# Token mixing in two halves of the features, interleaved with the output projection

## The chip, the cores and the metric

The kernel runs on one core of a Trainium2 chip. The metric is the device time of one execution in microseconds (us). Five engines work beside each other and meet at semaphores: TensorE (PE; its weight loads are listed as PEld), VectorE (DVE), ScalarE (ACT), GpSimd (POOL) and SyncE (SP), which issues DMAs.

## The reference

Three layers follow each other, for 4 batches of 576 tokens and 512 features (8 heads of 64):

```
scores = q @ k.T / sqrt(D) + min(-(cum[i] - cum[j]), 0), causal   # cum = cumsum(relu(s))
x      = softmax(scores) @ v                                      # heads side by side: (B, 576, 512)
gate   = sigmoid(causal conv of x over 5 tokens, per feature)
x      = (gate * (x @ w_val)) @ w_out
h      = x.T @ U @ V          # token mixing: U is 576 x 32, V is 32 x 576
u      = x + h.T
out    = u + relu(u @ w_ch1) @ w_ch2                              # 512 -> 2048 -> 512
```

Everything is float32. The large products are made of fp32r pieces: a value is split into a rounded high part and a rest, and three products (high with high, high with rest, rest with high) are added in PSUM.

## The kernel before, in words

Features lie on the partitions. uT holds the whole activation as 4 tiles of 128 features by 2304 tokens. The work has three stages. First attention: 32 heads in a software pipeline (the loop at line 762), scores of head n beside the transposes and products of head n - 1. After each pair of heads `norm` (590) scales the accumulator av, of which there is one buffer (pool psV), and five conv taps and a tanh (609 to 622) overwrite it and read it. Second, for each batch, `dense_work` (640): `values` (645) makes gate times the value projection, split into gvh and gvl per tile of 128 features and half of the tokens; `outputs` (668) makes the output projection and then the token mixing. Third, the two-layer MLP (865 to 933).

`outputs` first loops over the two halves of 288 tokens and, inside, over the 4 feature tiles m; each of these 8 output tiles is 12 matmuls of 288 columns (`products`, 627), and ACT writes it to uT (kind "ox"). Then comes token mixing, for the 5 chunks of 128 tokens (the last overlaps): four PE transposes bring the chunk of all 512 features into one PSUM bank (686 to 690), ACT rounds it to nh, DVE makes the rest nl, and two matmuls of 512 columns add U times nh and U times nl into the bank acc (699, 700). The sum is split into the tile `a` (named ast): ACT rounds it, DVE makes the rest of its lower half (703, 704). Last, 16 matmuls of 288 columns multiply with V, and DVE adds each result to uT (706 to 713). nh and nl have one buffer each, and ast uses nh's.

What sets the order: these functions are generators. Each `yield` names a cost on a planner's clock, and between two yields the caller puts other work. For batches 0 to 2 the caller is `run_dense` (751), which spreads a batch's dense work over the attention of the next batch, at a budget (DENSE = 36.0) divided by the heads that are left. For batch 3 it is `beside` (943), which puts 0.4 of a piece of the MLP's first blocks behind each yield and 6 pieces behind the yield of the value LULL. `defer` (156) emits a step some time later on that clock, `force` (160) at once; `until` (184) moves the clock on until a step has been emitted. At the end a list scheduler orders each engine's instructions by a simulated time and by priorities that the table PLAN (23) gives to each kind of step; the kind "tm" (the mixing's matmuls and transposes) goes 6000 places ahead. All matmul results of the three stages except av and two MLP accumulators share one pool of 6 PSUM banks, psD (225).

Of the kernel before, what the change touches and what calls it, by code (L numbers as in the profile page):

```python
# [11 lines left out]
F32 = mybir.dt.float32  # L12
F32R = mybir.dt.float32r
# [78 lines left out]
DT = {"exp": 0.51, "xh": 0.96, "xl": 0.25, "tap": 1.5, "taps": 0.9, "tanh": 1.83, "gv": 4.3, "nl": 3.6, "rows": 10.0, "prep": 1.51}  # L92
# [4 lines left out]
def fused_kernel(ctx, tc, qT, kT, vP, s, wval, wout, convw, U, V, w1, w2, rows01, out):  # L97
    nc = tc.nc
    B, H, D, S = qT.shape
    P = 128  # L100
    NP = H // 2
    NT = B * S
    HS = S // 2
# [31 lines left out]
    def rnd(kind, o, i, by=1.0):  # L135

        eng = Via(kind)
        if eng.name == "scalar":
            eng.mul(o, i, by)  # L139
        elif eng.name == "vector" and by == 1.0:  # L140
            eng.tensor_copy(o, i)
        else:
            eng.tensor_scalar(o, i, by, 0.0, op0=ALU.mult, op1=ALU.add)  # L143

    def rest(kind, o, i, hi, by=1.0):

        if by == 1.0:
            Via(kind).tensor_sub(o, i, hi.bitcast(F32))
        else:
            Via(kind).scalar_tensor_tensor(o, i, by, hi.bitcast(F32), op0=ALU.mult, op1=ALU.subtract)  # L150
# [5 lines left out]
    def defer(dt, f, key=None):  # L156
        order[0] += 1
        later.append((clock["now"] + dt, order[0], f, key))

    def force(key, keep=0):  # L160

        held = sorted((x for x in later if x[3] == key), key=lambda y: y[:2])
        for x in held[:max(0, len(held) - keep)]:
            later.remove(x)
            x[2]()
# [18 lines left out]
    def until(*keys):  # L184

        while any(k not in ready for k in keys):
            assert later
            advance(0.1)
# [12 lines left out]
    uT = left.tile([P, NP, NT], F32, name="uT")  # L201
# [425 lines left out]
    def products(o, w, m, hi, lo):  # L627

        K = len(hi)
        for kc in range(K):  # L630
            wh = w["h"][:, kc, m * P:(m + 1) * P]
            Via("d").matmul(o, wh, hi[kc], start=(kc == 0), stop=False)
            Via("d").matmul(o, wh, lo[kc], start=False, stop=False)
            Via("d").matmul(o, w["l"][:, kc, m * P:(m + 1) * P], hi[kc], start=False, stop=(kc == K - 1))
            yield 0.37
# [32 lines left out]
    def outputs(b):  # L668
        halves = [slice(0, HS), slice(HS, S)]
        need(*[("wide", c) for c in range(NP, 2 * NP)])  # L670
        for hf, cols in enumerate(halves):
            for m in range(NP):
                until(*[("gv", b, p, hf) for p in range(NP)])
                ps = psD.tile([P, 512], F32, tag="d", name="d")
                yield from products(
                    ps[:, 0:HS], wo, m, [gvh[p, hf] for p in range(NP)], [gvl[p, hf] for p in range(NP)],
                )
                rnd("ox", uT[:, m, b * S + hf * HS:b * S + hf * HS + HS], ps[:, 0:HS], 0.5)
        yield 0.0
        need(*[("wide", c) for c in range(2 * NP, len(wide))])  # L680
        acc = psD.tile([P, 512], F32, tag="d", name="d")
        for c in range(5):
            s0 = b * S + min(c * P, S - P)
            force("pt", 1)
            if b < B - 1:
                ps = psD.tile([P, 512], F32, tag="d", name="pt")
            else:
                ps = psD.tile([P, 512], F32, tag="d", name="d")
            for m in range(NP):
                Via("tm").transpose(ps[:, m * P:(m + 1) * P], uT[:, m, s0:s0 + P], ident)  # L690
            nh = da.tile([P, 512], F32R, tag="nh", name="nh")
            nl = da.tile([P, 512], F32R, tag="nl", name="nl")
            rnd("nh", nh, ps)
            defer(DT["nl"], lambda ps=ps, nh=nh, nl=nl: rest("nl", nl, ps, nh), "pt")
            yield 0.44
            yield 0.8
            force("pt")
            lhsT = U4[:, c, :, :].rearrange("p a r -> p (a r)")
            Via("tm").matmul(acc, lhsT, nh, start=(c == 0), stop=False)
            Via("tm").matmul(acc, lhsT, nl, start=False, stop=(c == 4))  # L700
            yield 0.44
        a = da.tile([P, 512], F32R, tag="nh", name="ast")
        rnd("ah", a, acc)
        rest("al", a[64:, :], acc[64:, :], a[64:, :])
        yield LULL
        for m in range(NP):
            for hf, cols in enumerate(halves):
                ps = psD.tile([P, 512], F32, tag="d", name="d")
                lhsT = a[:, m * P:(m + 1) * P]
                Via("tm").matmul(ps[:, 0:HS], lhsT, V4["h"][:, cols], start=True, stop=False)  # L710
                Via("tm").matmul(ps[:, 0:HS], lhsT, V4["l"][:, cols], start=False, stop=True)
                u = uT[:, m, b * S + hf * HS:b * S + hf * HS + HS]
                Via("um").tensor_add(u, ps[:, 0:HS], u)
                yield 0.25

# [299 lines left out]
```

## Time and profile before

| | us |
|---|---|
| median of 3 timed runs | 756.13 (754.95 to 756.43) |
| the profiled execution | 759.41 |
| its span, first to last instruction | 757.3 |

| engine | busy us | share of the span |
|---|---|---|
| PE | 733.2 | 97% |
| PEld | 617.8 | 82% |
| DVE | 473.0 | 62% |
| POOL | 337.8 | 45% |
| ACT | 264.5 | 35% |

Busy time is an average over stages that differ. By the instructions of the trace, attention runs up to about 319 us, the dense work of batch 3 from there to about 380 us, and the MLP alone after that. The ends of matmuls in a profile are modelled, so that a wait of PE can be somewhat longer than the idle time listed. The granted clock is given as a share of 2.4 GHz.

### The profile page before, as it was taken

The numbers are of one execution on the slowest core, as the hardware profiler recorded it, in microseconds if no ns is written. First come the engines' busy times: TensorE is split into PE (matmuls) and PEld (weight loads), VectorE is DVE, ScalarE is ACT, GpSimd is POOL, SyncE is SP. The second block draws the span as 40 slices with busy tenths as digits, with TensorE's granted clock in tenths as the row PEclk, the third lists the DMA queues.
The fourth block names the chain that finished last, engine by engine and source line by source line (L and its number), as shares of the span: only waits on it lengthen the run. The fifth ranks groups of instructions, "written<-read, shape, count | busy, mean of one in ns | idle before, by whom it ended". The sixth has DMA issues, their size and how long they took to land.

```text
span 757.3 us, 12161 instructions
## 1 busy us (share of the span) xinstructions
PE 733.2 (97%) x4369; PEld 617.8 (82%) x4369; DVE 473.0 (62%) x1053; ACT 264.5 (35%) x718; POOL 337.8 (45%) x393
## 2 busy tenths in 40 slices
PE   8988999899999999999999999999999999999998
PEld 5756889688887998798788888888888888888887
DVE  6888887987668656752548899864572234223234
ACT  6767656745677567622110110110011011001110
POOL 2677677555544243650097787732660024100000
PEclk9999999999999999999999999999999999999999
DMA  4665454645555431110002222210120000000033
GB/s 120 192 186 141 104 141 117 167 117 141 119 140 137 113 97 43 46 57 1 0 29 84 84 84 84 84 55 29 57 85 0 1 29 1 0 1 1 0 112 139
DMA packets 27000, 59.39 MB, mean 78 GB/s; under 512 B 4648, under 2 KB 5288, under 8 KB 26940
## 3 DMA queue, kind: packets, MB, share of 16 engines
q1 hardware_dynamic: 26940, 58.61, 27.8%
q8 instruction: 35, 0.57, 0.3%
q14 instruction: 25, 0.20, 0.1%
HBM read 37.04 MB, written 5.31 MB: 56 GB/s over the span
## 4 chain that ended last, share of the span: by engine, by line
PE 85%; DVE 8%; issue 2%; DMA 2%; ACT 2%; POOL 1%; ACTq 0%; DVEq 0%; POOLq 0%
PE d L132 39%; PE acc L132 26%; PE pt L132 8%; PE av L132 6%; PE sc L132 5%; DVE P L132 2%; DVE uT L132 2%; DVE av L614 2%; DMA uT<-in_w 1%; ACT P L132 0%; DMA K<-Q 0%; DVE nl L132 0%; POOL uT L143 0%; DVE uT L313 0%; ACT PTB L132 0%
## 5 line engine op out<-in xcount | busy, mean ns | idle before, releaser
L132 PE MATMUL d<-u,w1h 128*128 128x512 f32 (+1 forms) x640 | 184.4, 371 | 0.0
L877 ACT ACTIVATE hh<-d 128x512 fp32r<-128x512 f32 (+1 forms) x80 | 44.3, 556 | 342.8 <-PE acc L132 173.8
L132 DVE SCALAR_TENSOR_TENSOR hl<-d,hh 128x512 fp32r<-128x512 f32 (+1 forms) x80 | 50.5, 634 | 147.2 <-ACT hh L877 147.0
L132 PEld LDWEIGHTS d<-u,w1h 128*128 128x128 f32 x640 | 116.0, 188 | 22.4
L132 PE MATMUL d<-u,w1l 128*128 128x512 f32 (+1 forms) x320 | 118.5, 371 | 0.0
L132 PE MATMUL acc<-hl,w2h 128*128 128x512 f32 (+1 forms) x320 | 104.5, 370 | 0.0
L132 PE MATMUL acc<-hh,w2h 128*128 128x512 f32 (+1 forms) x320 | 104.3, 371 | 0.2 <-DVE uT L132 0.2
L132 ACT ACTIVATE P<-P,nm 128x576 f32<-128x576 f32 (+4 forms) x160 | 89.1, 560 | 36.9 <-DVE nm L132 36.3
L132 PE MATMUL acc<-hh,w2l 128*128 128x512 f32 (+1 forms) x320 | 101.1, 369 | 0.0
L132 PE MATMUL sc<-K,Q 68*128 68x288 f32 (+13 forms) x384 | 87.8, 343 | 2.3 <-ACT PTA L139 1.5
L132 DVE TENSOR_TENSOR uT<-acc,uT 128x512 f32<-128x512 f32 (+1 forms) x120 | 70.1, 628 | 31.6 <-PE acc L132 31.5
L132 DVE CUSTOM_DVE_ANT_0 P<-sc,causal 64x64 f32<-64x64 f32 (+4 forms) x160 | 64.9, 420 | 26.4 <-PE sc L132 22.3
L132 PE MATMUL pt<-ident,P 128*128 128x128 f32 x480 | 75.6, 282 | 5.0 <-ACT P L132 3.0
L132 PEld LDWEIGHTS sc<-K,Q 68*128 68x128 f32 (+2 forms) x384 | 62.8, 194 | 9.7 <-ACT PTA L139 2.0
L132 PEld LDWEIGHTS d<-u,w1l 128*128 128x128 f32 x320 | 60.3, 188 | 11.2
L132 PEld LDWEIGHTS acc<-hh,w2h 128*128 128x128 f32 x320 | 58.8, 188 | 11.5 <-issue 0.6
L132 PEld LDWEIGHTS acc<-hl,w2h 128*128 128x128 f32 x320 | 58.9, 188 | 10.9 <-DVE hl L132 0.3
L132 PEld LDWEIGHTS acc<-hh,w2l 128*128 128x128 f32 x320 | 58.7, 188 | 10.6
L132 PEld LDWEIGHTS pt<-ident,P 128*128 128x128 f32 x480 | 54.4, 142 | 13.5 <-ACT P L132 5.4
L132 DVE SCALAR_TENSOR_TENSOR scr<-raw,scr 128x512 uint32<-128x512 uint32 (+1 forms) x56 | 55.7, 995 | 1.4
L132 DVE TENSOR_SCALAR scr<-scr 128x512 uint32<-128x512 uint32 x56 | 44.7, 798 | 17.9 <-POOL scr L375 9.7
L614 DVE SCALAR_TENSOR_TENSOR av<-X,cw,av 128x576 f32<-128x576 f32 x64 | 52.1, 814 | 3.0 <-ACT av L132 2.7
(124 smaller groups left out, 1274.3 us busy)
## 6 DMA issues: line engine op xcount, KB each, us to landing
raw<-in_w SPq DMA_DIRECT2D x28, 512.0 KB
K<-hi SPq DMA_DIRECT2D x44, 144.0 KB
Q<-hi SPq DMA_DIRECT2D x44, 144.0 KB
V<-in_vP SPq DMA_DIRECT2D x16, 320.0 KB
out<-uT SPq DMA_DIRECT2D x16, 256.0 KB
qk<-in_qT SPq DMA_DIRECT2D x22, 144.0 KB
qk<-in_kT SPq DMA_DIRECT2D x22, 144.0 KB
K<-Q SPq DMA_DIRECT2D x22, 144.0 KB
```

The lines of the kernel that those rows point to most:

```text
L132: return f(*args, **kw)
L614: Via("tap").scalar_tensor_tensor(g, X[:, k:k + S], cw[:, p, k:k + 1], g, op0=ALU.mult, op1=ALU.add,)
L877: Via("hh").activation(h_, o, AF.Relu)
```

## The change

`outputs` becomes three inner generators: `output(m, hf)` for one output tile, `mix(f)` for the mixing of one half of the features (two tiles, 256 columns), and `back(f)` for that half's products with V. In `mix` two chunks of tokens share one PSUM bank of transposes and one tile nh and nl (chunks 0 and 1, 2 and 3, then 4 alone); the products with U take 256 columns each. Each half has its own tile ast. The output tiles of the first two feature tiles come first, for both halves of the tokens; the first mixing steps once behind every second product of the other four output tiles; the second mixing starts with three steps that yield nothing and then steps once behind each product pair of `back(0)`. The yield of LULL and `back(1)` come last. The second yield of a chunk costs 0.6 in place of 0.8.

```diff
@@ -668,50 +668,83 @@
     def outputs(b):
         halves = [slice(0, HS), slice(HS, S)]
         need(*[("wide", c) for c in range(NP, 2 * NP)])
-        for hf, cols in enumerate(halves):
-            for m in range(NP):
-                until(*[("gv", b, p, hf) for p in range(NP)])
-                ps = psD.tile([P, 512], F32, tag="d", name="d")
-                yield from products(
-                    ps[:, 0:HS], wo, m, [gvh[p, hf] for p in range(NP)], [gvl[p, hf] for p in range(NP)],
-                )
-                rnd("ox", uT[:, m, b * S + hf * HS:b * S + hf * HS + HS], ps[:, 0:HS], 0.5)
-        yield 0.0
+        def output(m, hf):
+            until(*[("gv", b, p, hf) for p in range(NP)])
+            ps = psD.tile([P, 512], F32, tag="d", name="d")
+            yield from products(
+                ps[:, 0:HS], wo, m, [gvh[p, hf] for p in range(NP)], [gvl[p, hf] for p in range(NP)],
+            )
+            rnd("ox", uT[:, m, b * S + hf * HS:b * S + hf * HS + HS], ps[:, 0:HS], 0.5)
+        W = NP // 2 * P
+        asts = {}
+        def mix(f):
+            ms = range(f * NP // 2, (f + 1) * NP // 2)
+            acc = psD.tile([P, 512], F32, tag="d", name="d")[:, 0:W]
+            for cs in ((0, 1), (2, 3), (4,)):
+                w = W * len(cs)
+                force("pt", 1)
+                if b < B - 1:
+                    ps = psD.tile([P, 512], F32, tag="d", name="pt")
+                else:
+                    ps = psD.tile([P, 512], F32, tag="d", name="d")
+                for k, (c, m) in enumerate((c, m) for c in cs for m in ms):
+                    s0 = b * S + min(c * P, S - P)
+                    Via("tm").transpose(ps[:, k * P:(k + 1) * P], uT[:, m, s0:s0 + P], ident)
+                nh = da.tile([P, 512], F32R, tag="nh", name="nh")
+                nl = da.tile([P, 512], F32R, tag="nl", name="nl")
+                rnd("nh", nh[:, 0:w], ps[:, 0:w])
+                defer(DT["nl"], lambda: rest("nl", nl[:, 0:w], ps[:, 0:w], nh[:, 0:w]), "pt")
+                yield 0.44
+                yield 0.6
+                force("pt")
+                for k, c in enumerate(cs):
+                    lhsT = U4[:, c, :, :].rearrange("p a r -> p (a r)")
+                    cols = slice(k * W, (k + 1) * W)
+                    Via("tm").matmul(acc, lhsT, nh[:, cols], start=(c == 0), stop=False)
+                    Via("tm").matmul(acc, lhsT, nl[:, cols], start=False, stop=(c == 4))
+                yield 0.44
+            a = asts[f] = da.tile([P, W], F32R, tag=f"ast{f}", name="ast")
+            rnd("ah", a, acc)
+            rest("al", a[64:, :], acc[64:, :], a[64:, :])
+        def back(f):
+            for k in range(NP // 2):
+                m = f * NP // 2 + k
+                for hf, cols in enumerate(halves):
+                    ps = psD.tile([P, 512], F32, tag="d", name="d")
+                    lhsT = asts[f][:, k * P:(k + 1) * P]
+                    Via("tm").matmul(ps[:, 0:HS], lhsT, V4["h"][:, cols], start=True, stop=False)
+                    Via("tm").matmul(ps[:, 0:HS], lhsT, V4["l"][:, cols], start=False, stop=True)
+                    u = uT[:, m, b * S + hf * HS:b * S + hf * HS + HS]
+                    Via("um").tensor_add(u, ps[:, 0:HS], u)
+                    yield 0.25
+        for hf in range(2):
+            for m in range(NP // 2):
+                yield from output(m, hf)
         need(*[("wide", c) for c in range(2 * NP, len(wide))])
-        acc = psD.tile([P, 512], F32, tag="d", name="d")
-        for c in range(5):
-            s0 = b * S + min(c * P, S - P)
-            force("pt", 1)
-            if b < B - 1:
-                ps = psD.tile([P, 512], F32, tag="d", name="pt")
-            else:
-                ps = psD.tile([P, 512], F32, tag="d", name="d")
-            for m in range(NP):
-                Via("tm").transpose(ps[:, m * P:(m + 1) * P], uT[:, m, s0:s0 + P], ident)
-            nh = da.tile([P, 512], F32R, tag="nh", name="nh")
-            nl = da.tile([P, 512], F32R, tag="nl", name="nl")
-            rnd("nh", nh, ps)
-            defer(DT["nl"], lambda ps=ps, nh=nh, nl=nl: rest("nl", nl, ps, nh), "pt")
-            yield 0.44
-            yield 0.8
-            force("pt")
-            lhsT = U4[:, c, :, :].rearrange("p a r -> p (a r)")
-            Via("tm").matmul(acc, lhsT, nh, start=(c == 0), stop=False)
-            Via("tm").matmul(acc, lhsT, nl, start=False, stop=(c == 4))
-            yield 0.44
-        a = da.tile([P, 512], F32R, tag="nh", name="ast")
-        rnd("ah", a, acc)
-        rest("al", a[64:, :], acc[64:, :], a[64:, :])
+        first = mix(0)
+        for hf in range(2):
+            for m in range(NP // 2, NP):
+                for i, cost in enumerate(output(m, hf)):
+                    yield cost
+                    if i % 2:
+                        yield next(first, 0.0)
+        yield from first
+        second = mix(1)
+        for _ in range(3):
+            yield next(second)
+        for cost in back(0):
+            yield cost
+            yield next(second, 0.0)
+        yield from second
         yield LULL
-        for m in range(NP):
-            for hf, cols in enumerate(halves):
-                ps = psD.tile([P, 512], F32, tag="d", name="d")
-                lhsT = a[:, m * P:(m + 1) * P]
-                Via("tm").matmul(ps[:, 0:HS], lhsT, V4["h"][:, cols], start=True, stop=False)
-                Via("tm").matmul(ps[:, 0:HS], lhsT, V4["l"][:, cols], start=False, stop=True)
-                u = uT[:, m, b * S + hf * HS:b * S + hf * HS + HS]
-                Via("um").tensor_add(u, ps[:, 0:HS], u)
-                yield 0.25
+        yield from back(1)
```

## Rows read from the trace of the kernel before

**Rows 1.** The page: PE's busy share, and the chain that ended last.
```profile
PE 733.2 (97%) x4369; PEld 617.8 (82%) x4369; DVE 473.0 (62%) x1053; ACT 264.5 (35%) x718; POOL 337.8 (45%) x393
...
PE 85%; DVE 8%; issue 2%; DMA 2%; ACT 2%; POOL 1%; ACTq 0%; DVEq 0%; POOLq 0%
```

**Rows 2.** Windows, columns as headed: outputs and mixing of batches 0 to 3.
```profile
core 0: us, PE busy (x) PEld busy (x) DVE busy (x) ACT busy (x) POOL busy (x), PEclk, DMA share, GB/s
...
131.90:160.90 29.00, 27.02 (x188) 20.60 (x186) 25.34 (x72) 19.04 (x55) 14.89 (x23) 0.94 0.58 148
188.60:215.90 27.30, 26.55 (x210) 24.55 (x209) 18.87 (x58) 18.22 (x55) 16.06 (x21) 1.00 0.46 113
215.90:242.00 26.10, 24.43 (x187) 19.59 (x186) 18.49 (x59) 18.59 (x55) 9.77 (x10) 1.00 0.58 138
268.00:294.00 26.00, 26.00 (x212) 24.55 (x211) 15.21 (x50) 18.31 (x55) 12.18 (x13) 1.00 0.36 84
294.00:319.20 25.20, 23.66 (x178) 18.30 (x176) 17.71 (x48) 16.02 (x46) 13.05 (x14) 1.00 0.05 15
...
348.90:380.40 31.50, 29.81 (x149) 24.06 (x148) 13.32 (x24) 6.21 (x11) 3.50 (x8) 1.00 0.00 1
```

**Rows 3.** The same view, inside the mixing of batch 0.
```profile
151.00:153.00 2.00, 2.00 (x13) 1.14 (x10) 1.90 (x6) 1.16 (x4) 1.01 (x2) 0.50 0.31 89
```

**Rows 4.** PE's waits, whole span: us in total, times, longest us.
```profile
PE pt L132 <- POOL wrs L132: 3.9, 2, 2.1
...
PE av L132 <- ACT uT L132: 2.7, 2, 1.5
PE d L132 <- DVE ast L148: 2.4, 2, 1.5
...
PE acc L132 <- DVE uT L132: 0.2, 1, 0.2
```

**Rows 5.** Timeline, batch 0: start us, us, engine, operation, [idle before <- releaser].
```profile
147.81 1.41 DVE L132 TENSOR_SCALAR uT<-uT 128x256 uint32<-128x256 uint32 x1
...
149.15 0.81 DVE L614 SCALAR_TENSOR_TENSOR av<-X,cw,av 128x576 f32<-128x576 f32 x1
...
149.99 0.65 ACT L132 ACTIVATE uT<-av 128x576 f32<-128x576 f32 x1 [0.29 <-DVE av L614]
...
150.69 2.19 PE L132 MATMUL av<-PTA,V 128*64 128x320 f32 x12 [1.47 <-ACT uT L132]
```

**Rows 6.** Timeline, batch 2.
```profile
311.08 0.60 ACT L132 ACTIVATE ast<-d 128x512 fp32r<-128x512 f32 x1
...
312.05 0.66 ACT L132 ACTIVATE uT<-av 128x576 f32<-128x576 f32 x1
...
312.46 0.40 PE L132 MATMUL d<-V4h,ast 128*128 128x288 f32 x1 [0.94 <-DVE ast L148]
```

**Rows 7.** Timeline, batch 3.
```profile
373.94 0.60 ACT L132 ACTIVATE ast<-d 128x512 fp32r<-128x512 f32 x1 [3.33 <-PE d L132]
374.57 0.69 DVE L148 TENSOR_TENSOR ast<-d,ast 64x512 fp32r<-64x512 f32 x1 [1.38 <-ACT ast L132]
...
375.32 0.40 PE L132 MATMUL d<-V4h,ast 128*128 128x288 f32 x1 [1.48 <-DVE ast L148]
```

**Rows 8.** The chain in order, MLP: start, us; 512 columns, then 256.
```profile
727.76 2.81 PE d L132 x12
...
745.05 1.42 PE d L132 x12
```

**Rows 9.** Weight loads of the products with U: ns min/median/max.
```profile
L132 PEld LDWEIGHTS d<-nh,U x20: 186/190/193, 135.6 to 370.7; 128*128 128x128 f32 x20
```

**Rows 10.** Groups by line and shape: count | busy us, mean ns | idle before.
```profile
L877 ACT ACTIVATE hh<-d 128x256 fp32r<-128x256 f32 x16 | 6.2, 385 | 53.4 <-PE acc L132 29.9 <-PE d L132 23.6
...
L713 DVE TENSOR_TENSOR uT<-d,uT 128x288 f32<-128x288 f32 x32 | 13.1, 449 | 3.6 <-PE d L132 3.6
...
L132 DVE TENSOR_TENSOR nl<-pt,nh 128x512 fp32r<-128x512 f32 x15 | 10.2, 682 | 2.0 <-ACT nh L139 2.0
...
L132 DVE TENSOR_TENSOR uT<-acc,uT 128x256 f32<-128x256 f32 x24 | 9.0, 415 | 0.9 <-PE acc L132 0.9
```

**Rows 11.** Windows, the last pair of heads beside the mixing, batches 0 to 2.
```profile
133.80:150.70 16.90, 14.92 (x112) 11.68 (x112) 15.24 (x38) 13.02 (x37) 10.25 (x14) 1.00 0.70 177
...
217.50:234.60 17.10, 15.53 (x113) 12.00 (x111) 12.39 (x37) 12.99 (x38) 6.93 (x7) 1.00 0.60 143
...
296.40:312.90 16.50, 15.01 (x110) 11.71 (x108) 11.78 (x31) 12.15 (x35) 7.75 (x9) 1.00 0.07 21
```

## The prediction

> **What bounds the kernel now.** I read the page's busy shares and chain first, then the stages one by one, then what TensorE (PE) waits for, then the instructions around its longest waits. PE is busy for 97% of the span and holds 85% of the chain [rows 1], so only two things can move the time: work that PE gains or loses, and the moments at which it stands still. The stages show where those are. In the output projections of batches 1 and 2 (the windows from 188.6 and 268.0) PE is idle for 0.75 us of 27.3 and for nothing of 26.0. In the four stages of token mixing (the other windows) it is idle for 29.00 - 27.02 = 2.0, 26.1 - 24.43 = 1.7, 25.2 - 23.66 = 1.5 and 31.5 - 29.81 = 1.7 us, 6.9 us in all [rows 2]. In the first of them the mean granted clock is 0.94, so another 29.0 x 0.06 = 1.7 us of full speed is lost there; the level inside is 0.50 of full, which is 1.2 GHz in place of 2.4 [rows 2, 3]. What PE waits for is named: the attention product (av) waits 2.7 us in two waits for the tanh on ScalarE (ACT), and the products with V (d) wait 2.4 us in two waits for the split of the mixed rows (ast) [rows 4].
>
> The instructions show two shapes. At the last pair of a batch, the accumulator av has one buffer, so PE cannot begin the next pair before the tanh has read it; the tanh follows the last conv tap on VectorE (DVE). In batch 0 that tap came at 149.15 because a 1.41 us step of a weight split stood ahead of it, and PE stood 1.47 us, after which the clock fell [rows 3, 5]. In batch 2 ACT ran the 0.60 us rounding of ast just ahead of the tanh, and the products with V waited 0.94 us for the second half of the split [rows 6]. In the last batch, with no attention beside it, PE ended the last mixing product and stood 1.48 us through an ACT rounding of 0.60 and a DVE rest of 0.69 [rows 7].
>
> **The change part by part.** One mixing of 512 features becomes two of 256. Per batch the PE transposes stay 20. The 10 products with U of 512 columns become 20 of 256, so four batches have 40 more matmuls and 40 more weight loads. Twelve matmuls of 512 take 2.81 us (234 ns each), twelve of 256 take 1.42 (118 ns each) [rows 8]: 80 x 118 - 40 x 234 = +0.1 us. Ends: nothing below (the same columns stream), and 40 x 190 ns = 7.6 us if no weight load were hidden [rows 9]. I take +0.2, since these rows are the same kind of matmul, run back to back with a weight load each. The Trainium skill (page "TensorE: Matmul & The Clock Gate", section "Back-to-back issue gap") speaks against the change here: it gives about 81 ns a matmul at 128 columns and 131 at 512 in a stream of load and matmul pairs, that is some 64 ns for every matmul whatever its width. By it the sum would hold an estimated 40 x 64 ns = +2.6 us more. The trace differs (118 ns against half of 234), and I go by the trace.
>
> ACT and DVE: five roundings and five rests of 512 become two halves of 512, 512 and 256, and each split of ast is done in two pieces of 256. A rest takes 682 ns at 512 and about 415 at 256, an ACT rounding 600 and about 385 [rows 7, 10]. Per batch DVE goes from 5 x 0.68 + 0.69 = 4.1 to 4 x 0.68 + 4 x 0.415 = 4.4 us, ACT from 3.6 to 4 x 0.60 + 4 x 0.385 = 3.9. Both have idle time in every stage [rows 2], so this costs nothing by itself; without that cover it would be 0.3 us a batch, 1.2 us in all.
>
> What moves. By the planner's costs a product of the projections counts 0.37, so the projection of value ends at 11.8 and that of the outputs at 23.7; the old mixing ran from there to 32.1 and the products with V, after a pause of 0.81, to 34.9. Now the first four output tiles end at 17.8, the first mixing lies beside the other four up to 28.1, its products with V lie beside the second mixing up to 32.1, then come the pause and the other four products, to 33.9. From the first old transposes (131.9) to the old ast (148.6) 8.4 of cost took 16.7 us, 2.0 us each. So half of the mixing moves some 12 us earlier, into stages in which PE hardly waits, and the second ast stands where the only one stood, at 32.1, but with half its width.
>
> What that is worth. If the mixing's stalls follow the number of chunks that still stand at the old place, half of 6.9 us goes: -3.4. From the other side, if only the width of the split matters, batch 3 saves (0.60 - 0.385) + (0.69 - 0.415) = 0.5, batch 2 the same, and batch 1 the 0.2 of ACT, 1.2 us in all. The end at which the new steps find no cover is +6.9 (the old stalls once more). I take -3.4 as the gross, and half of the clock's loss, -0.85, because the wait ahead of it has its cause in DVE's queue, which the change only partly empties.
>
> What is late next. Four more splits of ast stand in the way, the first of each batch. The four old ones cost 2.4 us of named waits [rows 4], 0.6 each; with half the width, and the transposes of the second mixing to run meanwhile, I take 0.3 each: +1.2 (0 if hidden, 2.4 if not). The adds of the first products with V (449 ns each [rows 10]) now come ahead of the last taps, not behind the split. In the last pair of a batch, DVE had five rests, 3.4 us. By the cost positions it now has the last rest of the first mixing 0.42, its split 0.42, rests of 0.68, 0.68 and 0.42, four adds 1.8 and the second split 0.42, which is 4.8: 1.4 us more in a stretch where it is busy 15.24 of 16.90 us in batch 0, 12.39 of 17.10 and 11.78 of 16.50 in the next two [rows 11]. ACT has less there, 2.7 us against 3.6 (five roundings and a split of 0.60 each). Behind the tap stand the tanh, then av on PE. I take 0.3 us a batch for three batches, +0.9 (0 to 1.4 each).
>
> The accumulator of the first mixing holds one of six PSUM banks through four output tiles, which take their banks from the same pool. No row shows the price of a bank; the outputs' 0.0 and 0.75 us of idle [rows 2] bound a loss from below, the mixing's 6.9 us from above, and I take nothing, as by the outputs. The order of outputs puts the second half of the tokens after two tiles in place of four; the split of gv must then be done 24 matmuls of 288 columns earlier. Eight tiles with attention beside them take 27.3 us [rows 2], so two still give it 7 us. I count nothing; a wait like the longest for ast would be 1.5 us [rows 4], and no gain can come of it.
>
> The sum: -3.4 - 0.85 + 0.2 + 1.2 + 0.9 = -1.95 us. The profiled execution took 759.4 us (span 757.3 and 2.1 around it), and would take 757.5. The median of the timed runs is 756.1, 3.3 lower, so I forecast 754.2 us.
>
> **The rivals.** (a) Slower: the adds and rests of the second half push the last taps back. For it speaks DVE at 90% in the last pair of batch 0, and that the wait there was already DVE's [rows 5, 11]; against it, batches 1 and 2 have 5 us of slack in the same place. If the 1.4 us show in full in each of three batches, and half of one more fall of the clock with them, while half of the gain comes, the time is 756.1 + 4.2 + 0.9 - 2.1 = 759.1. It decides where the last tap ends after PE's last score of the pair. (b) Nothing to see: the planner lets the mixing's matmuls go ahead of others as soon as they are ready, and had them spread among attention already; the waits come from roundings that take longer than planned, as often as before. For it speaks that of the 13 rows in the list of PE's waits, from the first shown to the last, none names a rounding or a rest of a chunk, only ast [rows 4]; then 1.2 us of width go and 0.9 to 1.2 come, 756.1. (c) Much faster: with shorter chains all mixing stages run like the outputs; 6.9 + 1.7 - 0.75 go, 0.2 comes, 748.5; against it, PE still meets a split of ast eight times. (d) A fixed price for each matmul shows: with half of the 7.6 us of weight loads exposed and the rest as forecast, 754.2 - 0.2 + 3.8 = 757.8. Against it speak the back-to-back times [rows 8]. By the page of the Trainium skill named above the estimate would be 756.6.
>
> **How the numbers follow.** A measurement of this kernel can tell about 0.2%, 1.5 us, from no change: faster is below 754.6, slower above 757.6. Chances: the forecast 0.41, with its own range from 751.5 to 755.0; (c) 0.09; (b) 0.26; (a) 0.20; (d) 0.04. Of the forecast's 0.41, 0.38 lies below 754.6 and 0.03 above; so faster has 0.38 + 0.09 = 0.47, no change 0.03 + 0.26 = 0.29, slower 0.20 + 0.04 = 0.24. The range from 749.0 to 759.5 leaves out part of (c) and the worst of (a), in which a second clock fall comes in full.
>
> **What would show it.** The products with V in two groups per batch, the first among the second mixing's transposes; in each mixing stage PE's idle near 1 us in place of 1.7; the wait for ast in the last batch near 1.0 us or gone; no half clock after 150 us. Wrong: av waiting for the tanh longer than 1.5 us, waits for nh or nl that were not there, or matmuls of 256 columns with U starting more than 130 ns apart back to back. If the stages before 103 us changed as well, the cause would not be one of these.

## The result: 1% slower, and where the microseconds stand

The changed kernel took 765.46 us (median of 4 runs, 761.21 to 770.95) beside 756.28 us for the kernel before (4 runs, 754.95 to 757.78): a ratio of 1.0108, 95% interval 1.0070 to 1.0145. Repeated on another chip with nine runs it took 763.37 us (760.37 to 768.84) beside 758.03: 1.0070 (1.0041 to 1.0099). So the change costs 5 to 9 us. Whether it also widens the spread from run to run is not shown: the first four runs lie 9.7 us apart beside 2.8 for the kernel before, but the nine later ones 8.5 us beside 9.0. The forecast was 754.2, with 759.5 as its upper end.

The page of after barely differs from [rows 1]. Its first line is busy time, the second the chain that ended last:

```profile
PE 734.9 (97%) x4409; PEld 622.1 (82%) x4409; DVE 473.5 (62%) x1061; ACT 266.0 (35%) x726; POOL 338.7 (45%) x393
...
PE 81%; DVE 11%; ACT 2%; DMA 2%; issue 2%; POOL 1%; SPq 0%; DVEq 0%; ACTq 0%; POOLq 0%
```

The 40 matmuls are there (x4409, in [rows 1] x4369). What moved is the chain: PE's part fell from 85% to 81%, DVE's rose from 8% to 11%. DVE is on the path more often, with no more work to do (473.5 us for 473.0).

The profiled executions differ by 2.2 us only (spans 759.5 and 757.3), since the first 76 to 80 us, which the change does not touch, happened to be 3.7 us shorter in after (the same instructions took from 75.3 to 79.6 us in the profiles below). So I cut the span at PE instructions that every timeline has: the first value product (d from xh) of each batch, the first output product (d from gvh) of batch 3, and the start of its last product with V. Stages in us, for every profile of this study:

| kernel | start | batch 0 | batch 1 | batch 2 | 3: values | 3: outputs, mixing | rest |
|---|---|---|---|---|---|---|---|
| before | 79.6 | 85.0 | 81.1 | 73.3 | 12.9 | 45.5 | 379.9 |
| after | 75.9 | 87.7 | 80.2 | 73.8 | 18.0 | 43.9 | 380.0 |
| again | 78.9 | 88.0 | 80.6 | 73.8 | 16.5 | 43.9 | 379.9 |
| b3only | 77.6 | 85.0 | 83.8 | 73.2 | 12.9 | 44.0 | 379.8 |
| b012 | 76.9 | 88.3 | 80.8 | 73.7 | 17.9 | 45.7 | 379.9 |
| lastrow | 76.2 | 94.1 | 79.8 | 74.1 | 12.9 | 43.9 | 380.2 |
| lastrow2 | 76.3 | 89.6 | 79.5 | 74.1 | 12.9 | 44.0 | 380.1 |
| b0old | 75.3 | 84.2 | 83.2 | 74.1 | 12.9 | 43.9 | 379.9 |
| split | 79.0 | 84.8 | 81.5 | 73.7 | 12.8 | 44.7 | 379.9 |
| umact | 78.0 | 86.9 | 80.1 | 74.1 | 12.9 | 43.9 | 379.9 |
| b13 | 75.3 | 83.8 | 81.7 | 73.3 | 13.2 | 44.0 | 379.9 |
| busy | 75.7 | 90.0 | 80.7 | 74.1 | 12.9 | 43.9 | 380.0 |
| bank | 76.6 | 90.9 | 81.3 | 75.5 | 12.9 | 45.6 | 380.5 |
| firstonly | 75.7 | 87.2 | 80.4 | 73.5 | 12.9 | 43.4 | 379.9 |

Over the five middle stages after is 303.6 - 297.8 = 5.8 us longer, and the repeat 5.0: +2.7 and +3.0 in batch 0, +5.1 and +3.6 in the values of batch 3, -1.6 in its outputs and mixing, -0.9 and -0.5 in batch 1, +0.5 in batch 2. Below are windows of after, with the columns of [rows 2]; its stages stand 1 to 4 us earlier than before's up to 319 us. The first of the two lines from 321 on is of before:

```profile
131.90:160.90 29.00, 25.85 (x180) 20.37 (x177) 22.46 (x63) 16.12 (x47) 16.02 (x23) 0.94 0.50 134
...
215.90:242.00 26.10, 25.47 (x203) 20.91 (x202) 18.31 (x60) 18.22 (x58) 8.96 (x9) 1.00 0.57 135
...
321.00:349.00 28.00, 28.00 (x194) 26.89 (x193) 13.77 (x28) 7.76 (x18) 13.25 (x16) 1.00 0.15 46
...
321.00:349.00 28.00, 25.27 (x166) 24.04 (x165) 14.16 (x29) 8.50 (x20) 12.58 (x15) 0.94 0.11 38
349.00:381.00 32.00, 31.54 (x170) 26.83 (x170) 13.36 (x25) 6.58 (x14) 2.85 (x6) 1.00 0.00 1
```

PE's idle time in batch 0's mixing went up, from 2.0 us [rows 2] to 3.15, in this pair of profiles (more on it below). In batch 1's it fell from 1.7 to 0.6, and in batch 3's from 1.7 to 0.5, as forecast. The window from 321 is a place that the prediction never looked at: PE was busy there for all 28.00 us in before; in after it stands for 2.7 us, and the mean clock of the window is 0.94.

PE's waits in after, columns as in [rows 4]:

```profile
PE pt L132 <- ACT P L132: 2.9, 6, 0.7
PE d L132 <- DVE gvl L148: 2.8, 2, 2.1
PE pt L132 <- POOL wrs L132: 2.6, 2, 1.8
PE pt L132 <- DVE nm L132: 2.3, 5, 0.7
...
PE d L132 <- DVE nl L132: 1.4, 2, 0.9
...
PE av L132 <- ACT uT L132: 0.9, 1, 0.9
```

The wait for ast (2.4 us in [rows 4]) is off the list, and av's wait for the tanh fell from 2.7 to 0.9. In their place stand gvl (the split of the gated values), nl (the rest of a chunk) and more of nm (the maximum of the softmax), all of them DVE's.

**Batch 3: the row sums came late.** The timeline of before where batch 3 begins, columns as in [rows 5]: the transposes of the last pair's row sums (pt from wrs) stand directly on both sides of the last av, and the tanh of that pair comes at 324.78.

```profile
316.52 0.49 PE L132 MATMUL pt<-ident,wrs 128*128 128x128 f32 x3
316.94 1.96 PE L132 MATMUL av<-PTB,V 128*64 128x192 f32 x20
318.82 0.44 PE L132 MATMUL pt<-ident,wrs 128*128 128x128 f32 x2
319.01 0.38 PE L132 MATMUL d<-xh,wvh 128*128 128x288 f32 x1
...
324.78 0.65 ACT L132 ACTIVATE uT<-av 128x576 f32<-128x576 f32 x1 [3.46 <-DVE av L614]
```

The same stretch of after:

```profile
316.25 1.15 PE L132 MATMUL av<-PTB,V 128*64 128x256 f32 x12
317.32 0.55 PE L132 MATMUL pt<-ident,wrs 128*128 128x128 f32 x3
317.62 0.38 PE L132 MATMUL d<-xh,wvh 128*128 128x288 f32 x1
...
322.31 0.29 PE L132 MATMUL d<-xh,wvl 128*128 128x288 f32 x1
322.44 0.38 PE L132 MATMUL pt<-ident,wrs 128*128 128x128 f32 x2
...
322.92 0.71 ACT L132 ACTIVATE wrs<-pt 128x320 f32<-128x320 f32 x2 [8.39 <-PE pt L132]
...
323.72 0.76 DVE L132 TENSOR_TENSOR X<-av,wrs 128x576 f32<-128x576 f32 x1 [7.42 <-ACT wrs L132]
...
325.29 2.54 DVE L614 SCALAR_TENSOR_TENSOR av<-X,cw,av 128x576 f32<-128x576 f32 x3 [0.81 <-ACT av L132]
327.74 1.18 DVE L132 SCALAR_TENSOR_TENSOR d<-uT,d 128x288 f32<-128x288 f32 x3
...
329.69 0.65 ACT L132 ACTIVATE uT<-av 128x576 f32<-128x576 f32 x1 [0.31 <-DVE av L614]
...
330.80 0.40 PE L132 MATMUL d<-xh,wvh 128*128 128x288 f32 x1 [2.15 <-DVE gvl L148]
```

Read it downwards: 4.8 us of value products slipped in between the first three transposes and the last two. ACT and DVE stood idle meanwhile (8.39 and 7.42 us), and the normalisation (X), the taps and the tanh came late, the tanh by 4.9 us, though the last av had ended 1.5 us earlier than in before. The gates (d from uT and d) and the splits of the gated values, which empty the value products' banks, stood among and behind the taps on DVE. PE stood 2.15 us for one of them. Two more windows show what follows: the clock is at 0.50, 1.2 GHz, and the 13 matmuls of a 2 us window become 10.

```profile
331.00:333.00 2.00, 2.00 (x13) 2.00 (x13) 2.00 (x7) 0.41 (x1) 0.33 (x1) 0.78 0.04 8
333.00:335.00 2.00, 2.00 (x10) 2.00 (x10) 1.97 (x5) 0.27 (x1) 0.00 (x0) 0.50 0.02 4
```

**Batch 0: short waits on DVE, and the clock.** The timeline of after that answers to [rows 5]:

```profile
141.21 0.66 PE L132 MATMUL pt<-ident,uT 128*128 128x128 f32 x4 [0.69 <-DVE nm L132]
141.67 1.52 DVE L132 SCALAR_TENSOR_TENSOR uT<-uT 128x256 uint32<-128x256 uint32 x1
143.12 0.44 DVE L724 TENSOR_TENSOR uT<-d,uT 128x288 f32<-128x288 f32 x1
143.48 0.81 DVE L614 SCALAR_TENSOR_TENSOR av<-X,cw,av 128x576 f32<-128x576 f32 x1
143.62 0.96 PE L132 MATMUL sc<-K,Q 68*128 68x448 f32 x4 [0.62 <-DVE uT L724]
...
146.58 0.41 PE L132 MATMUL d<-V4h,ast 128*128 128x288 f32 x1 [0.74 <-DVE nm L132]
...
147.97 0.58 PE L132 MATMUL d<-nl,U 128*128 128x256 f32 x1 [0.85 <-DVE nl L132]
```

In this stretch DVE works without a pause through weight splits (the 1.52 us step is one), taps, the softmax, rests and adds (L724; four adds now stand ahead of the end of the second half). PE stands four times for 0.6 to 0.85 us, until a step of DVE frees a bank or yields an operand; with the 0.26 at 144.95 that is the 3.15 us. In before it was one wait of 1.47 [rows 5] and shorter ones.

One pair of profiles does not show that these waits are a cost of the change. Over the whole of batch 0 PE is idle for 5.0 to 6.4 us in the five profiles that keep the old places there (before, b3only, b0old, b13, split) and for 5.8 to 6.8 in five with the new order (after, again, b012, lastrow, lastrow2). Waits for nl of 1.14 and 0.95 us stand in b3only and b0old, too. What differs is the clock: by the clock's records in the traces TensorE ran at half of it in or behind the mixing of batch 0 in all five of the new order (for 3.4, 3.4, 3.4, 17.1 and 10.2 us), and in one of the five others (before, 3.4 us). Batches 0 and 1 together, less half the length of such stretches, take 164.5 to 167.1 us in the old places and 164.0 to 167.3 in the new order.

### The profile page after: what moved, and what is told of

The parts are those of the page before. It is cut to its first block, busy times and chain, and to the rows that moved or that the text cites. A ratio compares the mean times of both kernels' runs of the same rounds, so it can differ in the third digit from the quotient of the medians.

```text
span 759.5 us, 12244 instructions
## 1 busy us (share of the span) xinstructions
PE 734.9 (97%) x4409; PEld 622.1 (82%) x4409; DVE 473.5 (62%) x1061; ACT 266.0 (35%) x726; POOL 338.7 (45%) x393
## 4 chain that ended last, share of the span: by engine, by line
PE 81%; DVE 11%; ACT 2%; DMA 2%; issue 2%; POOL 1%; SPq 0%; DVEq 0%; ACTq 0%; POOLq 0%
PE d L132 38%; PE acc L132 26%; PE pt L132 7%; PE sc L132 5%; PE av L132 5%; DVE uT L132 3%; DVE av L614 3%; DVE P L132 2%; DMA uT<-in_w 1%; ACT P L132 1%; DVE X L132 1%; DVE nl L132 0%; DMA qk<-in_kT 0%; DVE d L132 0%; DMA K<-hi 0%
## 5 line engine op out<-in xcount | busy, mean ns | idle before, releaser
L132 ACT ACTIVATE P<-P,nm 64x64 f32<-64x64 f32 (+4 forms) x160 | 89.3, 561 | 41.0 <-DVE nm L132 40.4
L132 PEld LDWEIGHTS sc<-K,Q 68*128 68x128 f32 (+2 forms) x384 | 60.8, 192 | 10.6 <-DVE nm L132 1.9
L132 DVE TENSOR_SCALAR scr<-scr 128x512 uint32<-128x512 uint32 x56 | 45.1, 805 | 17.1 <-POOL scr L375 9.0
```

The costliest lines, as they stand in the source:

```text
L132: return f(*args, **kw)
```

## The experiments

Three sets, each on one chip beside the kernel before: 758.03 us there in the first (26 runs), 758.15 in the second (35), 758.67 in the third (31). In each set the kernel before itself ran from 754 us to 762 and more. b3only, b012, b0old and b13 hold both forms of the token mixing and pick one by batch. Clock loss below is (1 - mean granted clock) x span, averaged over a kernel's runs: before 3.55, 3.4 and 2.9 us in the three sets, the changed kernel 7.5 in the first (9.6 in its four earlier runs). It is an estimate of what half clock cost, rather too high: among the runs of one kernel a microsecond of it goes with some 0.7 us of time.

**again** is the changed kernel once more.

> The changed kernel once more, to see where its runs part. Its first four runs lie at 761.2, 762.8, 768.1 and 771.0 us, with a mean granted clock of 0.993, 0.991, 0.984 and 0.982. Theory A (new waits in the stages of batches 0 to 2 and at the start of batch 3 let the clock fall, in some runs more often): 760 to 771 again, and a mean clock that goes down as the time goes up, some 1.7 us for each 0.0022 of it. Theory B (the new order costs PE itself a fixed time): all runs within 2 us of each other at the same clock.

763.37 us, +5.3; 18.0 us of values in the first profile, 16.5 in this one: the late row sums are no accident of one run. Both theories hold in part. The slower runs have the lower clock (theory A), though time rises by less than the 1.7 us for each 0.0022 that was expected, some 1.0 in these nine runs. Of the 5.5 us between the mean times 3.9 are clock loss and 1.6 are not (theory B).

**b3only** and **b012**: the new mixing in the last batch alone, or in the first three alone.

```
    def outputs(b):
        # b3only
        return outputs_new(b) if b == B - 1 else outputs_old(b)
        # b012
        return outputs_new(b) if b < B - 1 else outputs_old(b)
```

> The new order of projection and mixing in batch 3 only; batches 0 to 2 as before. Theory A (the cost is made in batches 0 to 2, whose mixing lies beside attention): 754 to 757, not slower than before, since the 1.48 us wait for ast in batch 3 is gone. Theory C (the loss is in batch 3, where the mixing's sum takes a PSUM bank beside the MLP's sums): 760 or more.

> The new order in batches 0 to 2 only; batch 3 as before. Theory A: as slow as the changed kernel or slower, 762 to 770, with the 2.1 us wait of the value products for gvl near 330 us and a stretch of half clock behind it. Theory C: 755 to 758.

b3only: 757.45 us, 0.9990 (0.9964 to 1.0017), with 44.0 us in batch 3's outputs and mixing for 45.5: the forecast gain there is real, 1.5 us, though the run times don't resolve it. b012: 765.12 us, 1.0081 (1.0049 to 1.0112), values 17.9, with the wait of 2.1 us for gvl that was expected. So the whole loss comes from the first three batches, also the part that shows in the last.

**lastrow** gives the row sums of the very last pair a higher priority than the products, and changes nothing else of after.

```
-    "t_rb": ("tensor", 500),
+    "t_rb": ("tensor", 500), "t_last": ("tensor", 20000),
...
-                Via("t_rb").transpose(ps[:, o:o + P], wide_rs[:, c, :], ident)
+                Via("t_rb" if pr < B * NP - 1 else "t_last").transpose(ps[:, o:o + P], wide_rs[:, c, :], ident)
```

> The changed kernel, with one edit: the five transposes of the last pair's row sums go ahead of the value products of batch 3, as they stood before; the order of PE before that point is the changed kernel's. If the late second half of these transposes (3.6 us after the first in the changed kernel's trace) is what holds the taps, the gate and so the banks of the value products, the 2.1 us wait near 330 us goes, and with it one stretch of half clock: 3 to 4 us less than the changed kernel. If the wait comes from DVE's or ACT's own queue there, nothing changes.

759.69 us, 1.0019 (0.9994 to 1.0045), 3.7 us under the changed kernel in the same set. (The late transposes start 5.1 us after the first three, not 3.6 as the expectation has it.) Its timeline has all five transposes behind the last av, its values stage is back to 12.9, and the wait of 2.1 us for gvl is gone (one of 0.6 is left, as in before):

```profile
321.75 1.96 PE L132 MATMUL av<-PTB,V 128*64 128x192 f32 x20
323.63 0.77 PE L132 MATMUL pt<-ident,wrs 128*128 128x128 f32 x5
324.15 0.38 PE L132 MATMUL d<-xh,wvh 128*128 128x288 f32 x1
```

So 3.7 of the 5.3 us were the row sums; by the mean times 1.5 us of this is clock loss. What is left is about all clock: lastrow's runs are on average 1.8 us longer than those of the kernel before (2.5 in lastrow2), and their clock loss is 2.4 us greater (4.1). In the profile it sits in batch 0, with the longest stretch at half the clock of the study (a run of 762.9 us, 3 above the median). Its windows there, and below the dots those of before:

```profile
137.00:149.00 12.00, 8.82 (x57) 7.03 (x57) 10.21 (x26) 6.88 (x20) 7.60 (x11) 1.00 0.48 130
149.00:155.00 6.00, 6.00 (x21) 4.58 (x20) 4.10 (x15) 4.68 (x15) 1.51 (x3) 0.52 0.51 137
155.00:161.00 6.00, 6.00 (x26) 4.08 (x24) 3.40 (x12) 1.14 (x3) 2.51 (x5) 0.50 0.00 1
...
149.00:155.00 6.00, 4.53 (x22) 2.97 (x21) 5.31 (x18) 2.87 (x9) 3.47 (x6) 0.72 0.52 141
155.00:161.00 6.00, 6.00 (x45) 4.50 (x44) 5.42 (x20) 2.66 (x7) 1.36 (x4) 1.00 0.28 67
```

PE counts as busy for all 12 us from 149 on, with 47 matmuls; before has 67 in the same 12 us, waits included. The experiments that follow ask what batch 0 costs and why; b0old, b13, umact and busy are built on lastrow.

**b0old** and **b13**: lastrow with the old mixing in batch 0, and in batches 0 and 2.

```
        # b0old
        return outputs_new(b) if b > 0 else outputs_old(b)
        # b13
        return outputs_new(b) if b in (1, B - 1) else outputs_old(b)
```

> The new order in batches 1 to 3, the old in batch 0, and the last pair's row sums ahead as in lastrow. Theory A (after the late row sums, what is left of the loss is batch 0's mixing): some 2.5 to 3 us less than lastrow's 759.7, so 1 to 2 us under the kernel before, whatever that runs at on this chip. If the rest of the loss is spread over the batches: 0.5 to 1 us less than lastrow.

> The new order in batches 1 and 3 only, row sums ahead. By the stages measured (first value products to first value products, or to the end of the products with V): batch 1 gains 0.5 to 0.9, batch 2 lost 0.5, batch 3's output and mixing gains 1.6. So 1.5 to 2.5 us under the kernel before, the fastest version; if the stages don't add up, as the kernel before.

756.90 us, 0.9992 (0.9970 to 1.0015), and 758.40, 1.0006 (0.9984 to 1.0029). Batch 0 returns to 84.2 and 83.8 us, and b0old's clock loss is 2.65 us where lastrow had 5.95. Against lastrow (1.0019, and 1.0031 in the third set; mean 1.0025) b0old is 0.3% lower, at the edge of what the intervals tell apart. Neither beats the kernel before, as both were expected to; in b13 batch 1 gains nothing (81.7 us for 81.1).

**split** halves the features and moves nothing: all eight outputs, then both mixings, then the products with V.

```
         for hf in range(2):
-            for m in range(NP // 2):
+            for m in range(NP):
                 yield from output(m, hf)
+        yield 0.0
...
+        yield from mix(0)
+        yield from mix(1)
         yield LULL
+        yield from back(0)
         yield from back(1)
```

> Only the halving: both mixings after all eight output tiles, both groups of products with V after them and the pause, nothing interleaved; two chunks share a bank, 40 more matmuls. If the matmuls of 256 columns and the additional roundings and splits cost anything, it shows here: PE's term of the prediction says +0.2, a fixed price of every matmul 2 to 4 us more than before. Theory A: within 1.5 us of before, batch 0's stage not longer than before's 85.0 us between the first value products of batches 0 and 1.

757.47 us, 0.9988 (0.9967 to 1.0009). The 40 matmuls and the doubled splits cost nothing that can be measured (at most 0.7 us by the interval); the loss lies in the places, not in the halves.

**umact** is lastrow with four of batch 0's steps at L724 moved from DVE to ACT; the sum with the old activation is left out there.

```
-                    Via("um").tensor_add(u, ps[:, 0:HS], u)
+                    if b == 0 and f == 0:
+                        nc.scalar.mul(u, ps[:, 0:HS], 1.0)
+                    else:
+                        Via("um").tensor_add(u, ps[:, 0:HS], u)
```

> As lastrow, but in batch 0 the first four results with V are written to the activation by ACT, in place of the add on DVE; the sum with the old activation is left out there. PE's order differs in some 40 rows inside batch 0's mixing. Theory A1 (PE waits in batch 0 since the adds, which free the banks of the results with V, stand in DVE's queue behind taps and weight splits): PE's idle time in the 12 us around the first products with V falls from 3.1 to under 1.6, and the time by 1.5 to 3 us against lastrow. Theory A2 (too few banks, or too many handoffs, whoever empties them): idle time and total as lastrow, within 1 us.

757.85 us, 0.9981 (0.9961 to 1.0001), clock loss 3.0 (before 3.4), and in its profile no stretch at half the clock from 77 us up to the end of the span. The time is what theory A1 forecast: 1.8 us under lastrow by the medians, some 3 by the ratios. Its mechanism is not: PE's idle should have fallen to under 1.6 us and did not. Windows of umact, to be held against those of lastrow above:

```profile
137.00:149.00 12.00, 9.20 (x70) 7.49 (x69) 10.02 (x22) 7.51 (x21) 8.29 (x12) 1.00 0.45 129
149.00:155.00 6.00, 5.85 (x36) 4.66 (x36) 5.74 (x22) 5.43 (x18) 2.91 (x4) 1.00 0.69 159
155.00:161.00 6.00, 4.97 (x48) 3.73 (x46) 3.63 (x11) 2.84 (x8) 2.67 (x5) 1.00 0.60 169
```

Idle from 137 to 161 is 3.98 us here and 3.18 in lastrow; the stage takes 86.9 us for 94.1 and 89.6, since the clock keeps its level. So with 4 x 0.44 = 1.8 us less on DVE ahead of the taps the waits stay and the loss of clock goes. The edit also moves some 30 rows in PE's order, so that DVE's queue as the cause is likely, but not shown alone.

**busy** is lastrow with 35 matmuls of 256 columns that nobody reads, put among the second mixing's transposes and the first products with V of batch 0. They fill some of PE's gaps and cost time elsewhere. **lastrow2** is lastrow beside it on the same chip.

```
+                if b == 0 and f == 1:
+                    for _ in range(5):
+                        Via("t").matmul(ps[:, 0:256], warm[:, 0:P], warm[:, 0:256], start=True, stop=True)
...
+                    if b == 0 and f == 0:
+                        for _ in range(5):
+                            Via("t").matmul(ps[:, 0:256], warm[:, 0:P], warm[:, 0:256], start=True, stop=True)
```

> As lastrow, but in batch 0 PE runs five more matmuls of 256 columns of zeros ahead of each of the three groups of transposes of the second mixing and of each of the four first products with V, 35 in all, some 3.8 us at full clock; their results are overwritten. Theory A3 (most of what batch 0's new waits cost is the half clock that follows them): mean granted clock 0.996 or more with less spread, no long stretch of half clock after 149 us, and 1 to 3 us less than lastrow in spite of the additional work. Theory A4 (the waits themselves cost, the clock adds little): the matmuls come on top where they don't fit a wait, 0 to 4 us more than lastrow.

> The kernel of lastrow once more, as the neighbour of the next one on the same chip: 758 to 761, with a mean granted clock that differs from run to run between 0.987 and 0.998, as it did there.

busy 759.04 us (757.2 to 760.6), lastrow2 759.89 (756.8 to 765.67). The clock loss falls from 6.97 us to 2.46, the spread (standard deviation) from 2.8 to 0.8 us; without the clock's part busy is 2.8 us longer. The windows of busy beside those of lastrow above: more busy time, and the clock at 1.00 throughout.

```profile
137.00:149.00 12.00, 9.74 (x84) 8.66 (x80) 9.19 (x22) 5.52 (x16) 7.54 (x11) 1.00 0.37 104
149.00:155.00 6.00, 5.94 (x46) 5.09 (x45) 5.96 (x23) 4.54 (x14) 3.89 (x6) 1.00 0.69 170
```

So theory A3 was right on the clock, not on the time: 0.85 us less by the medians in place of 1 to 3. As a remedy it gives back what it saves.

**bank** is the kernel before with one PSUM bank of batches 0 to 2 taken early and held through four output tiles, as the changed kernel holds its first sum.

```
+            if hf == 1 and b < B - 1:
+                acc = psD.tile([P, 512], F32, tag="d", name="d")
+                Via("tm").matmul(acc[:, 0:64], warm[:, 0:P], warm[:, 0:64], start=True, stop=True)
...
-        acc = psD.tile([P, 512], F32, tag="d", name="d")
+        if b == B - 1:
+            acc = psD.tile([P, 512], F32, tag="d", name="d")
```

> The kernel before; only the bank of the mixing's sum is taken earlier in batches 0 to 2, through the last four output tiles, by one matmul of 64 columns of zeros. It prices one bank of six held for the time that the first mixing's sum holds it in the changed kernel. The prediction's term: nothing (within 1 us of before). If banks are what makes batch 0's new waits: 2 to 4 us more.

764.28 us, 1.0077 (1.0051 to 1.0103): +5.6 us from nothing but a bank and one small matmul a batch, 2.9 of it clock loss. But the trace does not show PE waiting for a bank. From its timeline:

```profile
147.09 0.41 POOL L143 TENSOR_SCALAR uT<-uT 128x256 f32<-128x256 f32 x1 [4.09 <-DMA uT<-in_w]
...
148.02 1.48 DVE L132 TENSOR_SCALAR uT<-uT 128x256 uint32<-128x256 uint32 x1 [3.04 <-POOL uT L375]
149.41 0.81 DVE L614 SCALAR_TENSOR_TENSOR av<-X,cw,av 128x576 f32<-128x576 f32 x1
...
150.96 0.80 PE L132 MATMUL av<-PTA,V 128*64 128x320 f32 x2 [4.60 <-ACT uT L132]
```

A weight-split step whose transfer had not landed stood on DVE ahead of the last tap, so DVE stood 3.04 us, and PE 4.60 for the tanh behind it. In [rows 5] the same kind of step was there without the wait. The bank changed the order that the planner writes (some 65 of PE's rows, and some of every other engine), and SyncE issued that transfer some 66 us after the batch's first value product, in before some 64. That is where the price came from in this profile, by way of order and not of a wait for a bank.

**firstonly** is the changed kernel with the second mixing in one piece, and all products with V behind it; the first mixing stays beside the outputs, and its bank is held.

```
-        second = mix(1)
-        for _ in range(3):
-            yield next(second)
-        for cost in back(0):
-            yield cost
-            yield next(second, 0.0)
-        yield from second
+        yield from mix(1)
         yield LULL
+        yield from back(0)
```

> The first mixing beside the output tiles as in the changed kernel; the second mixing alone after it, then the pause, then all eight products with V as before; the last pair's row sums stand together here without an edit. Theory A1 (the first products with V, whose adds stand in DVE's queue beside the second mixing, make batch 0's waits): no loss in batch 0, 756.5 to 758.5, like split. If the first mixing beside the outputs makes them: like lastrow or slower, 759.5 to 762.

758.35 us, 0.9991 (0.9973 to 1.0010), values 12.9 without any change of priority. The time is as theory A1 forecast, its reason only in part: batch 0 still takes 87.2 us in its profile, without any half clock (batch 3's outputs and mixing 43.4), and the clock loss over the runs is 5.1 us, above before's 2.9. What it gains elsewhere makes up for that. So by the run times the net loss goes when the first products with V no longer stand among the second mixing; in which stage, one profile does not show. It also shows that a bank held by the first sum need not cost anything in total: the 5.6 us of bank cannot be carried over to the changed kernel.

## Why the prediction was wrong

**The step that failed first: no term for what the moved work displaces.** The prediction priced the mixing's own instructions and those of the last pairs beside them. The row sums of the last pair appear in none of its steps, and batch 3's value stage, busy for 28.00 of 28.00 us in before, is not even among the windows it read. That place cost 3.7 us (lastrow against the changed kernel), more than the whole gross gain of 3.4: waits of 2.7 us on PE in the profile of after, and half clock behind them.

A misreading stands close by. The prediction, and the account of the code ahead of it, say that three steps of the second mixing yield nothing. The code is `yield next(second)`: their costs, 1.48, do count. So the second ast stands at 33.6, not 32.1, and a batch's dense work ends at 35.4, not 33.9; before it ended at 34.9. The end of the dense work, which decides what competes with the last row sums and with the next batch's values, moved later and not earlier. No run separates this from the other changes of order.

**"Half of 6.9 us goes: -3.4."** Right where no attention stands beside the mixing: batch 3 gave 1.5 to 1.6 us (its wait for ast is gone, as forecast). Batch 1 gave 0.5 to 0.9. Batch 2 gave nothing (+0.5), and batch 0, the largest of the four, went the other way by 2.7 to 3.0 us in the two profiles, part of which comes back in batch 1.

**The step that failed second: "half of the clock's loss, -0.85".** The sign was wrong. The clock loss over the run rose from 3.5 to 7.5 us, and without the late row sums (lastrow, lastrow2) it is still 2.4 and 4.1 us above the kernel before. That is about all that these two lose (1.8 and 2.5 us by the means), so that the other terms together, -1.1 us in the sum, came to about nothing or a small gain. The prediction took one profile's one stretch at half the clock as the quantity, but it varies: 3.4 us of it in batch 0 in before and after, 10.2 and 17.1 in two profiles of the same kernel (lastrow).

**"What is late next", +1.2 and +0.9.** The four more splits of ast cost nothing that the waits name. The 0.9 for DVE has the engine right and the path not shown. This is rival (a), put at 0.20 and at 3.0 us above the kernel before; lastrow, the change without the row sums, lies 1.7 and 1.2 us above it by the medians. But the rival expected av to wait longer for a late tanh, and that wait fell to 0.9 us. In after PE waited for the softmax, an add and a rest in its place, the last being a wait for nl, one of the prediction's signs of being wrong, which b3only and b0old show as well. The waits of batch 0 add up to hardly more than in the old places (5.8 to 6.8 us for 5.0 to 6.4 in the profiles here); that the rival came near the time is luck. In batches 1 and 2 the slack that spoke against it was there.

**The bank, "I take nothing".** Not borne out by the experiment on it (bank: +5.6), yet firstonly, which holds the same bank, shows no loss. Whether the bank has any share in the changed kernel stays open, and the prediction's reason, the idle time of the outputs, says nothing on it, since the price came by way of order.

**"+0.2" for 40 matmuls, and rival (d).** Right. In after, matmuls of 256 columns with U start 120 ns apart where they stand together:

```profile
367.41 0.28 PE L132 MATMUL d<-nl,U 128*128 128x256 f32 x1
367.53 0.28 PE L132 MATMUL d<-nh,U 128*128 128x256 f32 x1
367.65 0.28 PE L132 MATMUL d<-nl,U 128*128 128x256 f32 x1
```

and split, which adds nothing but them and the splits, measured 0.9988. The estimate of +2.6 us worked out from the section "Back-to-back issue gap" of the Trainium skill's page "TensorE: Matmul & The Clock Gate" is not borne out: the interval of split ends at 1.0009, 0.7 us.

**What stays open.** Why the last two transposes fell behind the value products: a higher priority cures it, and so does the other order of firstonly, and PE had no idle time ahead of them, so the order was written that way. Whether the planner did so by priority or since it counted no bank as free is not shown. Why the new order in batch 0 brings more half clock at about the same idle time, and why it lasts 3.4 us in one profile and 17 in another. The first four runs of the changed kernel lie 2 us above the nine later ones, and their clock loss, 9.6 us for 7.5, accounts for it; why it was greater is open. No version here beats the kernel before beyond its interval.

## What to carry to other kernels

Where one engine is busy for 97%, moved work displaces something in every queue and pool that it passes: list what stands next in order at both its old and its new place, the next batch's first steps included, before counting the stalls it leaves behind. Waits on TensorE, even several of 0.6 to 0.85 us, have to be priced with the stretch at half its clock that can follow, which in these profiles lasted 3.4 to 17 us and cost up to half of that. One profile of the kernel before is a weak measure of a stage's waits: batch 0 with the old mixing had 5.0 us of idle in one and 6.4 in another. And read the generator's yields, not its comments: a cost that is passed on moves all that comes after.

## What the runs showed that I had not expected

The same instructions in the same order had stretches at 1.2 GHz of 17.1 us in one profile and 10.2 in another, both in batch 0 among waits that add up to 3.2 and 2.4 us, none longer than 0.84 (lastrow and lastrow2); PE's rows counted as busy all the while, so that only the granted clock and the number of matmuls in a window showed it. And 35 matmuls whose result nobody reads made the runs steadier (757.2 to 760.6 us for 756.8 to 765.7) at no cost in the median.
